# Top-k attention and a squared-ReLU FFN on one core: V laid out by head, a shorter way to the first scores, earlier evacuations in the last steps, and a reordered end

## The chip, the cores and the metric

The kernel runs on one core of one Trainium2 chip. The metric is device time in microseconds (us) of one launch. Of the kernel before there are three timed runs, and one more execution under the hardware profiler. The engines are TensorE (PE, matmuls and, as PEld, weight loads), VectorE (DVE), ScalarE (ACT), GpSimd (POOL) and SyncE (SP, which here issues DMAs).

## The reference

Eight batches of eight heads, 576 positions, 64 numbers per head. For each row of scores only the 32 largest count (and ties with the 32nd); the softmax over them weighs V. The result, 4608 tokens by 512, goes through an FFN with squared ReLU.

```python
scores = scale * np.matmul(q, k.transpose(0, 1, 3, 2))
kth = np.partition(scores, -top_k, axis=-1)[..., -top_k:-top_k + 1]
scores = np.where(scores >= kth, scores, -1000000000.0)
attn = np.exp(scores - np.max(scores, axis=-1, keepdims=True))
attn = attn / (np.sum(attn, axis=-1, keepdims=True) + 1e-09)
x = np.matmul(attn, v)            # then (B*S, H*D)
h = np.maximum(x @ w_in, 0.0)     # w_in 512 x 2048
out = h * h @ w_out               # w_out 2048 x 512
```

## The kernel before

**Units of work.** Heads are taken in 32 pairs, and a pair's 576 query rows in chunks of 128, 128, 128, 128 and 64. A *step* `u` treats one chunk of both heads of a pair, that is two tiles of 128 rows by 576 scores; the chunks of 64 rows of two pairs share a step. There are `U` = 144 steps. In the last batch the four pairs are taken chunk by chunk, so that its tokens come complete one chunk after the other.

**What a step does.** PE multiplies Q by K into the two PSUM tiles `sc_a` and `sc_b` (288 columns each; line 202), ACT copies them to `s` in SBUF (line 207). DVE takes the larger of each pair of columns (`split`, lines 238 to 243), PE brings a part of that back into `sc_b` through an identity matmul (`bring`, line 223), and DVE compares once more (`join`, line 250), so that later rounds look at short windows only. POOL makes the smaller ones by integer sums and differences (lines 257, 265, 269). DVE then finds the 32 largest in four rounds of eight: MAX8 (line 288) over 100, 120, 256 and 576 columns, and MATCH_REPLACE8 (line 292) after each of the first three. In the next step ACT makes `marks` (line 334: what lies below the 32nd) and, earlier, the exponentials `w_two` (`expo`, line 343, one instruction for each of the two tiles); POOL adds the marks to the exponentials as integers (`mask`, line 339); SP turns the result by a transposing DMA into `wT` (line 382); PE multiplies it by V with a column of ones (`weigh`, line 410); DVE inverts the sum (lines 415, 421), and ACT places the result in `x_tok` (line 438).

**Loads.** `load_pair` reads Q, K and V of a pair on SP's queue, one pair ahead of its use. Partition p holds rows 4p to 4p+3 of a head. The SBUF tiles are laid out `[128, chunk 5, head 2, 64]`: the four chunks of a row lie beside each other in DRAM (1 KB), but in SBUF the two heads alternate, so each piece written is 64 float32, 256 B. V's two tiles `v_raw_a` and `v_raw_b` are fixed; POOL casts them (line 154) to `vau`, where a column of ones stands behind each 64 numbers. `prep_units` makes a pair's Q and K ready in units: `main` (line 134) transposes four chunks of Q or K on PE and copies them scaled to `qkT` by ACT (line 138; the very first K by DVE, line 136), `rest` (line 146) does the 64 rows that remain, `values` the cast.

**FFN.** It is woven into the steps as pieces. An `up` (line 512) is a matmul group into one of two PSUM buffers `gen`; its `bend` evacuates by ACT's ReLU into `rl` (line 518) and squares it on POOL (line 526) or, through the list `later`, on ACT (line 523). A `down` (line 540) adds 16 products into `dn_ps`, which `leave` copies to `wide` (line 547) and stores. These evacuations wait in the list `late`; `flush()` issues whatever stands there, and `piece()` flushes before it takes a new piece. `idle_piece` (line 559) is a matmul group without a use, there to keep PE busy. From step `Z` = `U` - 19 on a step ends so:

```python
expo(u, 0)
if u == U - 4:
    piece()
    flush()
expo(u, 1)
flush()
```

**Order.** `pin` keeps each engine's instructions in the order of the program text; the times that `owe` books decide only whether POOL or ACT, DVE or POOL gets certain work.

**The end.** The last step has no later step behind which to hide. Its exponentials (`expo_last`, line 372) come before the 32nd value is known, DVE multiplies them by the comparison (`mask_last`, line 377), PE instead of a DMA transposes them (`turn_last`, lines 392, 395, 397), DVE places the result (`place_last`, line 904). The last 128 tokens get their FFN in quarters of the inner dimension (`x_last(kh)`, lines 884 and 886, and `ups_last(bank, kh)`, line 891, 8 matmuls for each half), collected in `sc_a` and `sc_b`, which are called `one` and `two` there; quarter kh is pair kh of the batch. The last quarter in the order is followed by ReLU (line 896), square (line 898), the `down` matmuls (line 966) and the store. `verify` and `note` (lines 304, 313 to 315) check that the rounds of eight found what they should; lines 947 to 950 sum that up in a flag for a general path, which is not taken here.

Of the kernel before, what the change touches and what calls it, by code (L numbers as in the profile page):

```python
# [22 lines left out]
def kernel(  # L23
# [83 lines left out]
    def load_pair(i):  # L107
        b, pr = pairs[i]
        got = []
        for name, src in (("q_raw", q), ("k_raw", k), ("v_raw", v)):  # L110
            t = ld.tile([128, 5, 2, 64], f32, name=name) if name != "v_raw" else v_raws[i % 2]
            queue = nc.scalar if i == 0 and name == "k_raw" else nc.sync
            two = src[b, 2 * pr:2 * pr + 2]
            if i < 2:
                for a in range(2):
                    pin(queue.dma_start(out=t[:, 0:4, a, :], in_=two[a, 0:512].rearrange("(p c) d -> p c d", c=4)))
            else:
                pin(queue.dma_start(out=t[:, 0:4], in_=two[:, 0:512].rearrange("a (p c) d -> p c a d", c=4)))
            pin(queue.dma_start(out=t[0:64, 4], in_=two[:, 512:576].rearrange("h p d -> p h d")))
            got.append(t)  # L120
        raw[i] = got

    def prep_units(i):
# [5 lines left out]
        def main(which, src):  # L129
            def go():  # L130
                very_first = i == 0 and which == 1
                tp = ps_one.tile([128, 512], f32, name="gen", bufs=2)
                for c in range(4):
                    pin(nc.tensor.transpose(tp[:, c * 128:(c + 1) * 128], src[:, c], id_f[:, :]))
                if very_first:
                    pin(nc.vector.tensor_scalar(qkT[:, which, 0:512], tp[:, :], scalar1=EACH, scalar2=None, op0=ALU.mult))
                else:
                    pin(nc.scalar.activation(qkT[:, which, 0:512], tp[:, :], AF.Copy, scale=EACH))
                    owe(A=0.5)
            return go  # L140
# [10 lines left out]
        def values():  # L151
            owe(G=0.76)
            assert i < 6 or av_left[i - 6] == 0
            pin(nc.gpsimd.tensor_copy(va[:, :, :, 0:64], v_raw[:, :]))
# [494 lines left out]
    scores(0)  # L649
    split(0)  # L650
# [26 lines left out]
    for u in range(Z):  # L677
# [94 lines left out]
    for u in range(Z, U - 2):  # L772
# [40 lines left out]
        if u == U - 4:  # L813
            piece()
            flush()
# [58 lines left out]
    bend()  # L874
    square()
# [12 lines left out]
    def up_last(hp, f0, khs):  # L888
        for kh in khs:
            for n in range(4):  # L890
                pin(nc.tensor.matmul(out=hp[:, n * 128:(n + 1) * 128], lhsT=w_in[:, kh, (f0 + n) * 128:(f0 + n + 1) * 128],
                                     rhs=xl[:, kh, :], start=False, stop=(kh == 2 and n == 3)))
# [26 lines left out]
    bend()  # L919
    square()  # L920
# [179 lines left out]
```

## Time and profile before

| | us |
|---|---|
| Median of three runs | 868.44 |
| Lowest and highest run | 867.41, 871.32 |
| The profiled execution, its own time | 870.59 |
| Its span, first to last instruction | 868.8 |
| First of the 19 last steps (its first exponential) | 735.7 |
| Last MAX8 of DVE ends | 848.2 |
| Last store issued (SP) | 862.75 |

The profile covers one execution. A page of it gives busy time by engine, the chain of work that ended last and the costliest groups of instructions; views of the trace give single instructions in order of time, groups by line, waits, and busy time in chosen stretches. A group's row names line, engine, operation, output and inputs (partitions x elements, type), then count, busy us, mean ns of one, and idle time before it with the instruction that ended it. L288 is line 288 of the kernel.

### The profile page before, as it was taken

How to read it: one execution, taken by the hardware profiler on the slowest of the kernel's cores; microseconds unless marked ns; L12 is line 12 of the kernel's file. 1: busy time of each engine (PE TensorE's matmuls, PEld its weight loads, DVE VectorE, ACT ScalarE, POOL GpSimd, SP SyncE). 2: the span in 40 equal slices, each digit the busy share in tenths (PEclk: the TensorE clock that was granted, in tenths of full speed). 3: DMA queues.
4: the chain of work that ended last, by engine and by line, in shares of the span. 5: the costliest groups of instructions: out<-in, count | busy, mean ns of one | idle time of the engine just before them, and what ended most of it. 6: DMA issues, size and time to landing. Idle time of an engine off the chain costs nothing.

```text
span 868.8 us, 20017 instructions
## 1 busy us (share of the span) xinstructions
PE 761.5 (88%) x6038; PEld 484.6 (56%) x6038; DVE 837.7 (96%) x3427; ACT 810.6 (93%) x1635; POOL 797.5 (92%) x748
## 2 busy tenths in 40 slices
PE   6998997888888988889889888889898998999986
PEld 3554555555555545556555555556555654666654
DVE  5999999999999999999999999999999999999994
ACT  2887999999999999999999999999999999999982
POOL 3788999999999999999999999999999998999761
PEclk8999999999999999999999999999999999999998
DMA  5597776546556666356554565654565545423341
GB/s 122 125 228 156 185 172 109 121 101 114 95 106 114 120 120 121 67 112 121 109 120 96 113 115 98 124 116 105 114 128 109 117 100 107 87 58 86 73 84 44
DMA packets 325444, 98.06 MB, mean 113 GB/s; under 512 B 317520, under 2 KB 317776, under 8 KB 325328
## 3 DMA queue, kind: packets, MB, share of 16 engines
q1 hardware_dynamic: 323984, 96.28, 54.5%
q8 instruction: 49, 0.80, 0.4%
q14 instruction: 67, 0.55, 0.2%
q10 hardware_dynamic: 1344, 0.43, 0.2%
HBM read 36.70 MB, written 9.44 MB: 53 GB/s over the span
## 4 chain that ended last, share of the span: by engine, by line
DVE 56%; issue 12%; POOL 12%; PE 12%; ACT 7%; DMA 1%; SPq 0%; DVEq 0%; ACTq 0%; POOLq 0%
DVE m L288 25%; DVE cat L292 15%; DVE tops L238 7%; DVE cat L250 6%; POOL cat L257 5%; POOL cat L265 3%; ACT s L207 2%; PE sc_b L223 2%; PE sc_b L202 2%; PE gen L512 1%; POOL cat L269 1%; PE av_ps L410 1%; PE dn_ps L559 1%; ACT h L523 1%; PE dn_ps L540 1%
## 5 line engine op out<-in xcount | busy, mean ns | idle before, releaser
L288 DVE MAX8 m<-cat 128x8 f32<-128x100 f32 (+3 forms) x1152 | 435.1, 419 | 0.1
L292 DVE MATCH_REPLACE8 cat<-m,cat 128x100 f32<-128x100 f32 (+2 forms) x864 | 259.3, 308 | 0.3 <-issue 0.3
L265 POOL TENSOR_TENSOR cat<-s 128x576 int32<-128x576 int32 (+1 forms) x144 | 196.1, 1362 | 7.4 <-ACT s L207 7.1
L257 POOL TENSOR_TENSOR cat<-cat,tops 128x576 int32<-128x576 int32 (+1 forms) x144 | 196.0, 1361 | 1.9 <-DVE tops L238 0.8
L202 PE MATMUL sc_b<-qkT 64*128 64x288 f32 (+1 forms) x640 | 119.0, 449 | 33.7 <-DVE cat L250 24.3
L540 PE MATMUL dn_ps<-w_out,h 128*128 128x512 bf16 x560 | 143.3, 381 | 1.9 <-ACT wide L547 1.9
L223 PE MATMUL sc_b<-tops,id_f 128*128 128x144 f32 x528 | 96.6, 306 | 50.5 <-ACT s L207 50.2
L512 PE MATMUL gen<-xT,w_in 128*128 128x256 bf16 (+1 forms) x1088 | 128.5, 264 | 1.9 <-ACT rl L518 1.2
L512 PEld LDWEIGHTS <-w_in 128*128 128x128 bf16 x1344 | 109.9, 98 | 32.8 <-issue 19.9
L223 PEld LDWEIGHTS sc_b<-tops,id_f 128*128 128x128 f32 x528 | 73.4, 189 | 93.8 <-ACT s L207 90.3
L410 PEld LDWEIGHTS <-wT 128*128 128x128 bf16 (+3 forms) x1600 | 98.1, 99 | 47.0 <-issue 8.5
L334 ACT ACTIVATE marks_a<-s,m 128x576 bf16<-128x576 f32 x144 | 115.8, 812 | 0.0
L334 ACT ACTIVATE marks_b<-s,m 128x576 bf16<-128x576 f32 x142 | 110.4, 783 | 0.0
L202 PE MATMUL sc_a<-qkT 64*128 64x288 f32 (+1 forms) x640 | 109.1, 420 | 0.9 <-DVE tops L238 0.9
L207 ACT ACTIVATE s<-sc_b 128x576 f32<-128x576 f32 x144 | 94.8, 659 | 14.0 <-PE sc_b L202 8.6
L207 ACT ACTIVATE s<-sc_a 128x576 f32<-128x576 f32 x144 | 95.9, 666 | 6.6 <-PE sc_a L202 3.8
L238 DVE TENSOR_TENSOR tops<-sc_a,s 128x576 f32<-128x576 f32 x132 | 98.5, 746 | 0.0
L540 PEld LDWEIGHTS <-h 128*128 128x128 bf16 x560 | 47.7, 98 | 68.6 <-issue 31.3
L250 DVE TENSOR_TENSOR cat<-sc_b,tops 128x288 f32<-128x288 f32 x191 | 80.8, 443 | 5.2 <-PE sc_b L223 4.7
L518 ACT ACTIVATE rl<-gen 128x512 f32<-128x512 f32 x140 | 83.9, 599 | 1.0 <-PE gen L512 0.9
L202 PEld LDWEIGHTS sc_b<-qkT 64*128 64x128 f32 (+1 forms) x640 | 48.3, 176 | 61.6 <-DVE cat L250 33.2
L269 POOL TENSOR_TENSOR cat<-tops 128x288 int32<-128x288 int32 x97 | 77.8, 802 | 0.0
(133 smaller groups left out, 1358.4 us busy)
## 6 DMA issues: line engine op xcount, KB each, us to landing
out_dram<-wide SPq DMA_DIRECT2D x31, 256.0 KB, 2.7
q_raw<-in_q_dram SPq DMA_DIRECT2D x30, 256.0 KB, 3.7
k_raw<-in_k_dram SPq DMA_DIRECT2D x30, 256.0 KB, 3.7
h<-in_moe_w_in_dram SPq DMA_DIRECT2D x8, 512.0 KB, 5.3
h<-in_moe_w_out_dram SPq DMA_DIRECT2D x8, 512.0 KB, 4.2
v_raw_a<-in_v_dram SPq DMA_DIRECT2D x15, 256.0 KB, 4.1
v_raw_b<-in_v_dram SPq DMA_DIRECT2D x15, 256.0 KB, 4.0
out_dram<-wide SPq DMA_DIRECT2D x9, 128.0 KB, 2.5
```

The costliest lines, as they stand in the source:

```text
L202: pin(nc.tensor.matmul(out=sc[j][r if rest else slice(0, 128), x, 0:HALF], lhsT=qkT[r, 0, c * 128:min(S, (c + 1) * 128)], rhs=qkT[r, 1, j ...
L207: pin(nc.scalar.activation(s[:, :, j * HALF:(j + 1) * HALF], sc[j][:, :, 0:HALF], AF.Copy))
L223: pin(nc.tensor.matmul(out=far[:, x, :], lhsT=id_f[:, :], rhs=st[w]["tops"][:, x, QUAR:HALF], start=True, stop=True))
L238: pin(tt(tops[:, :, :], one, two, op=ALU.max))
L250: pin(nc.vector.tensor_tensor(d["cat"][:, :, lo:lo + QUAR], far, d["tops"][:, :, 0:QUAR], op=op))
L257: pin(nc.gpsimd.tensor_tensor(at, at, top, op=ALU.subtract))
L265: pin(nc.gpsimd.tensor_tensor(at, s[:, :, 0:n], s[:, :, HALF:HALF + n], op=ALU.add))
L288: pin(nc.vector.max(out=m[r][:, x, :], in_=cat[:, x, at]))
L292: pin(nc.vector.match_replace(out=cat[:, x, at], in_to_replace=m[r][:, x, :], in_values=cat[:, x, at], imm_value=NEG))
L334: pin(nc.scalar.activation(marks[u % 2][:, x, :], d["s"][:, x, :], AF.Relu, bias=d["m"][3][:, x, 7:8], scale=-1.0))
L512: pin(nc.tensor.matmul(out=hp[:, n * n_rows:(n + 1) * n_rows], lhsT=w_in[:, kh, (f0 + n) * 128:(f0 + n + 1) * 128], rhs=xt(kh), start=(kh ...
L540: pin(nc.tensor.matmul(out=op[:, :], lhsT=held["h2"][:, f, c * 128:(c + 1) * 128], rhs=w_out[:, f, :], start=(f == 0), stop=(f == NF - 1)))
```

## The change

It has four parts.

1. V's two tiles become `[128, head 2, chunk 5, 64]`, and a load writes the four chunks of a head as one piece of 1 KB. `values` reads the tile through a rearranged view in the old order.
2. For the first pair, `main` of Q is split: chunk 0 comes first, then K, `rest` and the cast, and chunks 1 to 3 follow the first scores. An `idle_piece` is added in step 0.
3. In the steps from `Z` on, the `flush` between the two exponentials, which was there in one step only, is in all.
4. At the end, both bends that are still open are issued ahead of the last step; the inverse for pair 1 goes between the last two rounds of the last step; `x_last((1,))` and its matmuls, `verify` and `note` go forward; pair 2 comes before pair 3; and quarter 3 instead of quarter 2 is the last.

```diff
-    v_raws = [const.tile([128, 5, 2, 64], f32, name=f"v_raw_{i}") for i in "ab"]
+    v_raws = [const.tile([128, 2, 5, 64], f32, name=f"v_raw_{i}") for i in "ab"]
     for t in v_raws:
-        nc.gpsimd.memset(t[64:128, 4], 0.0)
+        nc.gpsimd.memset(t[64:128, :, 4, :], 0.0)
...
-            t = ld.tile([128, 5, 2, 64], f32, name=name) if name != "v_raw" else v_raws[i % 2]
+            t = ld.tile([128, 5, 2, 64], f32, name=name) if name != "v_raw" else v_raws[i % 2][:, :, :, :].rearrange("p a c d -> p c a d")
...
+                if name == "v_raw":
+                    pin(queue.dma_start(out=v_raws[i % 2][:, :, 0:4, :], in_=two[:, 0:512].rearrange("a (p c) d -> p a c d", c=4)))
+                else:
+                    pin(queue.dma_start(out=t[:, 0:4], in_=two[:, 0:512].rearrange("a (p c) d -> p c a d", c=4)))
...
-        def main(which, src):
+        def main(which, src, c0=0, c1=4):
...
-                for c in range(4):
+                at = slice(c0 * 128, c1 * 128)
+                for c in range(c0, c1):
...
-            return [main(0, q_raw), main(1, k_raw), lambda: rest((1,), sc[0][:, 0, :]), values, lambda: rest((0,))]
+            return [main(0, q_raw, 0, 1), main(1, k_raw), lambda: rest((1,), sc[0][:, 0, :]), values, main(0, q_raw, 1, 4), lambda: rest((0,))]
...
     scores(0)
+    soon.pop(0)()
     split(0)
...
+        if u == 0:
+            idle_piece()
...
         expo(u, 0)
         if u == U - 4:
             piece()
-            flush()
+        flush()
         expo(u, 1)
...
-    bend()
-    square()
+    for _ in range(2):
+        bend()
+        square()
     empty(two)
...
     expo_last(0)
     expo_last(1)
-    bend()
-    square()
     ups_last(one, 0)
     ups_last(two, 0)
     downs.pop(0)()
-    topk(u, (2, 3))
-    invert(u - 2)
+    topk(u, (2,), lambda: invert(u - 2))
+    topk(u, (3,))
     place(u - 2)
+    x_last((1,))
     mask_last(0)
     mask_last(1)
+    verify(u)
+    note()
     turn_last(0)
+    ups_last(one, 1)
     turn_last(1)
-    x_last((1,))
+    products(u - 1)
     st[u]["o"] = ps_one.tile([128, 512], f32, name="gen", bufs=2)[:, 0:130].rearrange("p (x d) -> p x d", x=2)
     products(u)
-    products(u - 1)
+    invert(u - 1)
+    place_last(u - 1)
     invert(u)
     place_last(u)
-    invert(u - 1)
-    place_last(u - 1)
-    x_last((3,))
-    ups_last(one, 1)
     x_last((2,))
     ups_last(two, 1)
-    ups_last(one, 3)
-    ups_last(two, 3)
-    verify(u)
-    note()
+    x_last((3,))
+    ups_last(one, 2)
+    ups_last(two, 2)
...
-        ups_last(bank, 2)
+        ups_last(bank, 3)
```

More of the change, by code (lines that the diff above doesn't have):

```diff
@@ L132, in go @@
                 tp = ps_one.tile([128, 512], f32, name="gen", bufs=2)
[L133 removed]
+                at = slice(c0 * 128, c1 * 128)
+                for c in range(c0, c1):
                     pin(nc.tensor.transpose(tp[:, c * 128:(c + 1) * 128], src[:, c], id_f[:, :]))
                 if very_first:
[L136 removed]
+                    pin(nc.vector.tensor_scalar(qkT[:, which, at], tp[:, at], scalar1=EACH, scalar2=None, op0=ALU.mult))
                 else:
[L138 removed]
+                    pin(nc.scalar.activation(qkT[:, which, at], tp[:, at], AF.Copy, scale=EACH))
                     owe(A=0.5)
@@ L891, in up_last @@
                 pin(nc.tensor.matmul(out=hp[:, n * 128:(n + 1) * 128], lhsT=w_in[:, kh, (f0 + n) * 128:(f0 + n + 1) * 128],
-                                     rhs=xl[:, kh, :], start=False, stop=(kh == 2 and n == 3)))
+                                     rhs=xl[:, kh, :], start=False, stop=(kh == KH - 1 and n == 3)))
     def square_last(z, bank):
```

3 lines of the change are left out of this document (1 added, 2 removed).

## The prediction

> **What bounds the kernel now.** I read the page first: which engine is busy, and how evenly. VectorE (DVE) leads, with ScalarE (ACT) and GpSimd (POOL) close behind.
>
> ```profile
> span 868.8 us, 20017 instructions
> ...
> PE 761.5 (88%) x6038; PEld 484.6 (56%) x6038; DVE 837.7 (96%) x3427; ACT 810.6 (93%) x1635; POOL 797.5 (92%) x748
> ```
>
> A busy share is a mean over stages, so the second view is busy time by stretch. Behind the length of a stretch each row gives busy us and instructions of PE, PEld, DVE, ACT and POOL, then the granted TensorE clock, the DMA share and GB/s.
>
> ```profile
> 0.00:10.00 10.00, 7.35 (x27) 3.51 (x27) 0.84 (x2) 2.75 (x4) 3.85 (x23) 1.00 0.67 144
> ...
> 100.00:600.00 500.00, 435.80 (x3447) 277.76 (x3448) 498.80 (x2054) 492.61 (x993) 495.04 (x455) 1.00 0.57 113
> 735.00:806.00 71.00, 67.54 (x574) 45.65 (x574) 66.07 (x274) 68.07 (x144) 69.57 (x64) 0.98 0.35 72
> 806.00:848.20 42.20, 38.78 (x380) 25.09 (x380) 41.98 (x182) 37.08 (x78) 29.48 (x30) 1.00 0.39 84
> 848.20:868.80 20.60, 12.09 (x121) 9.46 (x119) 8.40 (x19) 5.19 (x14) 2.09 (x4) 0.87 0.14 40
> ```
>
> From 100 to 600 us DVE is idle for 500 - 498.80 = 1.2 us: nothing is to be won there without taking DVE work away, and the change takes none. DVE's idle time lies in three places: the first 10 us (9.2 us), 735 to 806 us (71 - 66.07 = 4.9 us) and behind 848.2 us (20.6 - 8.4 = 12.2 us). Set beside the old one, engine by engine, the new order of instructions differs in just these places, and in the shape of V's loads. So there are four parts.
>
> **V in pieces of 1 KB: nothing.** Instruction groups (count | busy us, mean ns | idle before), then DMA issues (count, KB, median us to landing):
>
> ```profile
> L607 POOL CAST w_in<-h 128x1024 bf16<-128x1024 f32 x5 | 5.2, 1039 | 0.0
> ...
> L154 POOL CAST vau_a<-v_raw_a 128x640 bf16<-128x640 f32 x6 | 4.4, 727 | 3.5 <-DMA v_raw_a<-in_v_dram 3.5
> ```
> ```profile
> out_dram<-wide SPq DMA_DIRECT2D x31, 256.0 KB, 2.7
> ...
> v_raw_b<-in_v_dram SPq DMA_DIRECT2D x15, 256.0 KB, 4.0
> ```
>
> A store of 256 KB in rows of 2 KB lands in 2.7 us, a load of V in pieces of 256 B in 4.0 us: at best each load lands 1.3 us sooner. The one wait for V in the profile is POOL's 3.5 us ahead of its first cast, before POOL has other work, and load_pair runs a pair ahead. That lead is the cover; without it each of the 32 pairs could win those 1.3 us, or lose up to a landing. I take 0. The cast (L154) now reads in nested steps (chunk, head, 64 numbers) where it read 640 numbers in a row. From the two casts above, 384 more numbers cost 312 ns, 0.8 ns each, so 640 come to 0.52 us and 0.2 us is fixed; the output of L154 is in runs of 64 already and shows no price for them. I take the new cast at 0.73 us too; the bounds are that and double (a rival, below).
>
> **The start: -0.55 us.** Timeline rows: start us, length us, engine, line, and in brackets the idle time before and what ended it.
>
> ```profile
> 6.04 1.02 PE L134 MATMUL gen<-id_f,q_raw 128*128 128x128 f32 x4 [0.28 <-DMA q_raw<-in_q_dram]
> ...
> 6.90 0.60 PE L134 MATMUL gen<-id_f,k_raw 128*128 128x128 f32 x4
> ...
> 7.54 0.69 DVE L136 TENSOR_SCALAR qkT<-gen 128x512 f32<-128x512 f32 x1 [7.54 <-PE gen L134]
> ...
> 9.85 0.47 DVE L240 TENSOR_TENSOR sc_b<-sc_a,s 128x288 f32<-128x288 f32 x1 [1.62 <-ACT s L207]
> ...
> 11.13 0.65 ACT L207 ACTIVATE s<-sc_a 128x576 f32<-128x576 f32 x1 [1.32 <-DVE cat L243]
> ...
> 15.45 1.33 PE L202 MATMUL sc_b<-qkT 64*128 64x288 f32 x4 [2.28 <-ACT qkT L149]
> ...
> 18.46 0.47 DVE L240 TENSOR_TENSOR sc_b<-sc_a,s 128x288 f32<-128x288 f32 x1 [0.39 <-ACT s L207]
> ```
> ```profile
> L134 PE MATMUL gen<-id_f,k_raw 128*128 128x128 f32 x128 | 20.7, 284 | 0.6 <-ACT rl L518 0.6
> ```
> ```profile
> 14.00:21.00 7.00, 5.50 (x17) 2.49 (x18) 6.61 (x26) 2.06 (x4) 3.17 (x4) 0.53 0.56 126
> ```
>
> K's four transposes now stand behind one of Q's instead of four. Q's four took (6.90 - 6.04) / 4 = 0.215 us apiece; K's four took 0.60 with one of them lasting 0.28, so a step of (0.60 - 0.28) / 3 = 0.11: the clock rose in between. Three fewer are 0.645 us if K's keep their pace, but they would now run before the rise: four steps of 0.215 and 0.28 for the fifth end at 7.18 instead of 7.50, 0.32 sooner. I take 0.35, since the rise seems to go by time; the bounds are 0.32 and 0.645. All behind it (L136, the scores, L207, DVE's first L240) moves along. The other three transposes and their copy by ACT (384 columns, under the 0.60 us of 512) go behind the first scores, into the 1.32 us for which ACT waits ahead of its copy at 11.13: free; without that gap up to 0.6.
>
> The added idle_piece (four matmuls of 512) lands in the 2.28 us for which PE waits before 15.45: free up to that. It may keep the clock up through 14 to 21 us, where the mean was 0.53 and the scores took 1.33 us. Then DVE's 0.39 us at 18.46 goes. I take 0.2, bounds 0 and 0.39.
>
> **The last 19 steps: -1.2 us.** A flush now comes between the two exponentials in every step, so the waiting evacuation (L518 or L547) precedes the second one.
>
> ```profile
> 735.73 1.44 ACT L343 ACTIVATE w_two_c<-s,low 128x576 bf16<-128x576 f32 x2
> ...
> 737.08 0.57 ACT L547 ACTIVATE wide<-dn_ps 128x512 f32<-128x512 f32 x1
> ...
> 737.71 1.86 PE L559 MATMUL dn_ps<-fill,id_h 128*128 128x512 bf16 x4 [0.58 <-ACT wide L547]
> ...
> 742.91 0.46 DVE L250 TENSOR_TENSOR cat<-sc_b,tops 128x288 f32<-128x288 f32 x1 [0.47 <-PE sc_b L223]
> ...
> 751.02 1.03 PE L512 MATMUL gen<-xT,w_in 128*128 128x256 bf16 x8 [0.59 <-ACT rl L518]
> 751.05 1.04 POOL L526 TENSOR_TENSOR h<-rl 128x512 bf16<-128x512 f32 x1 [0.44 <-ACT rl L518]
> ...
> 755.73 0.82 DVE L250 TENSOR_TENSOR cat<-sc_b,tops 128x288 f32<-128x288 f32 x2 [0.69 <-PE sc_b L223]
> ```
> ```profile
> 800.96 1.02 PE L540 MATMUL dn_ps<-w_out,h 128*128 128x512 bf16 x4 [0.64 <-ACT wide L547]
> ...
> 805.61 0.82 DVE L250 TENSOR_TENSOR cat<-sc_b,tops 128x288 f32<-128x288 f32 x2 [0.93 <-PE sc_b L223]
> ```
>
> Three times PE waits for an evacuation behind the second exponential (0.58, 0.59, 0.64 us), then scores late, and DVE waits at its next L250 (0.47, 0.69, 0.93). The evacuation comes one exponential, 0.72 us, sooner; each stall shrinks by the smaller number, together 0.47 + 0.59 + 0.64 = 1.7 us. The second exponential is 0.6 us later. Behind it on ACT are the placing and the marks; POOL's addition to the weights waits for the marks, which end when they did, since the order only rotates ACT's work. That is the cover; without it the turn, and PE's products, would be 0.6 us late. But POOL is idle for only 71 - 69.57 = 1.4 us of this stretch and ACT for 2.9: they can take the bound over. I take 1.2, bounds 0 and 1.7.
>
> **The tail: -2.0 us.** The first row has the shortest, median and longest of two instructions, in ns.
>
> ```profile
> L377 DVE SCALAR_TENSOR_TENSOR w_two_c<-s,m,marks_b x2: 797/1196/1594, 848.2 to 848.9; 128x576 bf16<-128x576 f32 x2
> ```
> ```profile
> 846.26 1.04 POOL L526 TENSOR_TENSOR h<-rl 128x512 bf16<-128x512 f32 x1
> ...
> 848.59 1.31 POOL L526 TENSOR_TENSOR h<-rl 128x512 bf16<-128x512 f32 x1 [1.29 <-ACT rl L518]
> ...
> 850.57 0.45 PE L392 MATMUL gen<-id_h,w_two_c 128*128 128x128 bf16 x5 [1.06 <-DVE w_two_c L377]
> ...
> 853.60 0.29 PE L884 MATMUL gen<-id_h,x_tok 128*128 128x128 bf16 x1
> 853.68 1.06 PE L891 MATMUL sc_b<-xT,w_in 128*128 128x128 bf16 x8
> 854.53 1.06 PE L891 MATMUL sc_a<-xT,w_in 128*128 128x128 bf16 x8
> ...
> 857.21 1.08 ACT L896 ACTIVATE rl<-sc_a 128x512 f32<-128x512 f32 x2 [3.01 <-PE sc_a L891]
> ```
> ```profile
> 847.09 0.61 PE L891 MATMUL sc_b<-xT,w_in 128*128 128x128 bf16 x8
> ```
> ```profile
> 850.00:853.40 3.40, 2.47 (x35) 1.95 (x35) 1.79 (x6) 0.79 (x3) 0.00 (x0) 1.00 0.00 0
> 853.40:856.80 3.40, 3.40 (x34) 3.21 (x32) 1.89 (x6) 0.29 (x2) 0.78 (x3) 0.50 0.00 0
> ```
>
> mask_last(1) took 1.594 us beside POOL's square of 848.59, mask_last(0) 0.797. With both bends ahead of the last step that square follows the one of 846.26 and ends at 846.26 + 2 x 1.04 = 848.3, so the second mask should take 0.80 too: 0.8 us, and the transposes of 850.57 wait that much less. The new order then lets pair 2's product run while DVE copies the last transposed weights, and puts one group of eight L891 into PE's 1.06 us wait and a second between the two x_tok transposes: three groups, not four, stand between the last L884 and the first ReLU (L896). A group takes 854.53 - 853.68 = 0.85 us at half clock. Of that and the reordering I count 0.65 (the second group may hold up the last L884 by 0.3), so 0.8 + 0.65 = 1.45 us at half clock. At full clock eight take 0.61 in place of 1.06 (row of 847.09), so three groups win 3 x 0.45 = 1.35 more: 2.8. Between 1.45 and 2.8 no row decides: PE is busier than before, yet the clock fell after 3.4 us in which PE was busy for 2.47. I take 2.0. The flag checks move forward; DVE does them while PE runs L891, as before.
>
> The Trainium skill, page "TensorE: Matmul & The Clock Gate", section "Part 1: The HAM clock gate (the "warmup" mystery)", says that the clock is halved after an idle window of some 3.4 us, whose phase varies from run to run. The row of 850 to 853.4 us speaks against a wholly idle window as the condition; by the page the tail would keep its clock, as in the second rival.
>
> **Sum.** 0.55 + 1.2 + 2.0 = 3.75 us off the profiled execution's own 870.59 us (span 868.8 and 1.8 around it) are 866.84. That execution is 2.15 us above the median of the three runs, 868.44; against the median the forecast is 864.7 us.
>
> **Rivals.** First, the engines behind take over: POOL and ACT are the bound in the last 19 steps (for it, 69.57 of 71 us; against it, two of POOL's waits there are for the same L518) and the clock falls as before. 0.35 + 0 + 1.45 = 1.8 us: 866.6. Second, the clock stays full in both places: 0.35 + 0.39 + 1.2 + 2.8 = 4.7 us: 863.7. Third, slower: the nested read makes POOL's cast cost double. From 100 to 600 us POOL is idle for 500 - 495.04 = 5 us, over some 20 casts 0.25 us each; past that POOL becomes the bound, and 0.73 - 0.25 = 0.48 us on some 25 casts of the filled stage cost 12 us: 868.44 - 3.75 + 12 = 876.7. Against it is the price of runs of 64 above. That the 1 KB pieces do nothing for the time is no rival but part of all four.
>
> **How the numbers follow.** Forecast 0.45, first rival 0.22, second 0.20, third (with any other loss) 0.13. Lowest sum of all bounds: 1.03 + 1.7 + 2.8 = 5.5 us; three runs spread by some 2 us to each side. Range 861 to 869.5: from below the second rival to no gain at all with that spread; the third is left out. Half a per cent (4.3 us, about what a measurement of this kernel can tell from no change) lies at 864.1, just past the forecast. Faster by more: 0.65 of the second rival and half of the forecast's cases, 0.35; slower 0.12; the rest, 0.53, within.
>
> **What would show it.** K's transposes end near 7.2 us and DVE's first L240 starts near 9.5. The three L250 waits are below 0.4 us together with their PE waits gone; if POOL's idle time there falls to nothing while DVE's stays at 4.9, the first rival holds. Both L377 take 0.8 us; L896 starts 1.4 to 2.8 us sooner against the end of the last maximum. L154 stays at 0.73 us: above 1 us the third rival holds. A DVE idle time above 1.2 us between 100 and 600 us would prove the forecast wrong.

## The result, and the profile after

| | before | after |
|---|---|---|
| median of five runs each, side by side | 869.83 us (867.41 to 871.32) | 865.07 us (864.59 to 865.77) |
| ratio, 95% interval | | 0.9946 (0.9924 to 0.9968) |
| later, on one chip: 18 and 7 runs | 870.13 us (866.79 to 873.70) | 864.81 us (863.57 to 865.31) |
| ratio, 95% interval | | 0.9931 (0.9908 to 0.9955) |
| span of the profiled execution | 868.8 us | 863.3 us |

The change makes the kernel faster by 4.8 to 5.3 us. The forecast was 864.7 us. Lines behind the change have moved: old L134, L136, L154, L202, L207, L223, L240, L250, L377, L410, L518 and L896 are L138, L140, L158, L206, L211, L227, L244, L254, L381, L414, L522 and L904 in the changed kernel.

The page of the changed kernel, its head and the busy times, and then the same stretches as before, cut at the new end of the last maximum:

```profile
span 863.3 us, 19942 instructions
...
PE 754.1 (87%) x5960; PEld 483.8 (56%) x6042; DVE 836.9 (97%) x3427; ACT 810.0 (94%) x1636; POOL 797.2 (92%) x748
```
```profile
0.00:10.00 10.00, 7.19 (x26) 3.46 (x27) 0.86 (x2) 2.43 (x4) 3.85 (x23) 0.89 0.66 146
100.00:600.00 500.00, 431.71 (x3401) 277.93 (x3445) 498.64 (x2052) 492.09 (x992) 494.76 (x455) 1.00 0.55 113
735.00:806.00 71.00, 67.08 (x585) 46.32 (x594) 67.78 (x279) 69.51 (x148) 70.67 (x65) 1.00 0.38 74
806.00:846.80 40.80, 37.33 (x356) 23.82 (x359) 40.62 (x178) 35.87 (x76) 29.60 (x30) 1.00 0.44 88
846.80:863.30 16.50, 10.32 (x119) 7.97 (x119) 7.41 (x17) 4.61 (x12) 0.78 (x3) 0.94 0.26 46
```

Between 100 and 600 us nothing moved (DVE busy for 498.64 us, 498.80 before). From 735 to 806 us DVE, ACT and POOL are all busier, so the same work takes less time. The last stretch is 16.5 us long where it was 20.6. In the first 10 us the mean clock is given as 0.89, where it was 1.00, but these two cannot be compared: the time ahead of the clock's first rise counts as full in them. The rise came at 6.86 us before and at 4.45 us after, and the ten matmuls of the warm-up show it, first in the kernel before and then in the changed one (0.43 us from one to the next ahead of the rise, 0.21 behind it):

```profile
1.31 4.45 PE L620 MATMUL dn_ps<-fill 128*128 128x512 bf16 x10 [1.31 <-POOL fill L73]
```
```profile
1.31 3.86 PE L624 MATMUL dn_ps<-fill 128*128 128x512 bf16 x10 [1.31 <-POOL fill L73]
```

The timeline of DVE at the start of the changed kernel (only instructions behind a wait), and the clock by windows of 3.41 us, show what comes behind the rise:

```profile
6.78 0.69 DVE L140 TENSOR_SCALAR qkT<-gen 128x512 f32<-128x512 f32 x1 [6.78 <-PE gen L138]
9.84 0.47 DVE L244 TENSOR_TENSOR sc_b<-sc_a,s 128x288 f32<-128x288 f32 x1 [2.36 <-PE sc_a L206]
14.30 0.47 DVE L244 TENSOR_TENSOR sc_b<-sc_a,s 128x288 f32<-128x288 f32 x1 [0.89 <-PE sc_a L206]
19.16 0.47 DVE L244 TENSOR_TENSOR sc_b<-sc_a,s 128x288 f32<-128x288 f32 x1 [0.18 <-ACT s L211]
```
```profile
4.45:7.86 3.41, 1.91 (x12) 1.03 (x11) 0.69 (x1) 0.50 (x2) 0.59 (x1) 1.00 0.84 186
7.86:11.27 3.41, 2.69 (x11) 1.39 (x9) 1.43 (x4) 1.33 (x3) 0.17 (x2) 0.50 0.68 174
11.27:14.69 3.42, 2.79 (x10) 1.56 (x11) 2.54 (x16) 1.09 (x2) 1.58 (x2) 0.50 0.05 11
14.69:18.10 3.41, 3.36 (x13) 1.61 (x10) 3.41 (x12) 1.25 (x3) 1.59 (x2) 0.50 0.07 16
```

DVE's copy of K (L140) starts at 6.78 us, 0.76 sooner than the 7.54 of before. But the clock falls to half at 7.9 us and stays there for three windows, and DVE's first L244 is where it was (9.84 against 9.85); the third is 0.7 us later (19.16 against 18.46). From step 3 on, the two executions are level (0.02 us apart). The gain of the start is gone.

At the other end, rows of the last 19 steps and of the tail of the changed kernel, from the timelines of DVE, PE, ACT and SP's DMA queue:

```profile
804.05 0.82 DVE L254 TENSOR_TENSOR cat<-sc_b,tops 128x288 f32<-128x288 f32 x2 [0.27 <-PE sc_b L227]
...
846.68 1.53 DVE L381 SCALAR_TENSOR_TENSOR w_two_c<-s,m,marks_b 128x576 bf16<-128x576 f32 x2
...
849.37 0.79 PE L414 MATMUL av_ps<-vau_a,wT 128*128 128x65 bf16 x10 [0.65 <-DMA wT<-w_two_b]
...
853.14 1.08 ACT L904 ACTIVATE rl<-sc_a 128x512 f32<-128x512 f32 x2 [1.12 <-PE sc_a L899]
...
858.68 0.34 SPq L979 DMA_DIRECT2D out_dram<-wide  x1
```
The masks and the last store's issue of the kernel before, from the same timelines:

```profile
848.20 2.31 DVE L377 SCALAR_TENSOR_TENSOR w_two_c<-s,m,marks_b 128x576 bf16<-128x576 f32 x2
...
862.75 0.33 SPq L973 DMA_DIRECT2D out_dram<-wide  x1
```

From the first mask to the last store's issue it took 862.75 - 848.20 = 14.55 us and now takes 858.68 - 846.68 = 12.00 us; the two masks together take 1.53 us in place of 2.31. The ReLU at 853.14 (L904) was at 857.21 (L896). By stages, with the start of the first maximum of a step as the mark, the two profiled spans (868.81 and 863.30) part like this:

| stretch | before | after | difference |
|---|---|---|---|
| to the last 19 steps (step 125) | 731.38 | 731.67 | +0.29 |
| steps 125 to 142 | 107.69 | 105.84 | -1.85 |
| step 142 to the first mask | 9.13 | 9.17 | +0.04 |
| first mask to the last store's issue | 14.55 | 12.00 | -2.55 |
| last store's issue to the end | 6.06 | 4.62 | -1.44 |

The first row is not the start. The two executions stay level up to step 23; the difference comes at step 24, during a window of half clock from 151.2 to 154.6 us that only the changed kernel's execution has. (Steps 20 to 29 take 57.60 or 57.61 us in the six profiles here without a fall near 150 us, and 57.82 to 57.93 us in the eight with one.) The last row is no part of the change: in other profiles of the kernels here it lies between 4.6 and 5.8 us, with no pattern. V's casts and landings, a group and a DMA row of the changed kernel:

```profile
L158 POOL CAST vau_a<-v_raw_a 128x640 bf16<-128x640 f32 x6 | 4.3, 724 | 3.5 <-DMA v_raw_a<-in_v_dram 3.5
```
```profile
v_raw_b<-in_v_dram SPq DMA_DIRECT2D x15, 256.0 KB, 3.8
```

The nested read costs the cast nothing (724 ns against 727), and pieces of 1 KB land 0.2 us sooner (3.8 against 4.0), which nothing waits for.

So the time agrees with the forecast while its terms do not: the start gained nothing where 0.55 us were forecast, and the rest gained more. What the order did and what the clock did is the question for the runs.

### The profile page after: what moved, and what is told of

Its sections match the earlier page's. It is cut to its first block, busy times and chain, and to the rows that moved or that the text cites. A ratio compares the mean times of both kernels' runs of the same rounds, so it can differ in the third digit from the quotient of the medians.

```text
span 863.3 us, 19942 instructions
## 1 busy us (share of the span) xinstructions
PE 754.1 (87%) x5960; PEld 483.8 (56%) x6042; DVE 836.9 (97%) x3427; ACT 810.0 (94%) x1636; POOL 797.2 (92%) x748
## 4 chain that ended last, share of the span: by engine, by line
DVE 53%; PE 17%; issue 11%; POOL 11%; ACT 6%; DMA 1%; SPq 0%; DVEq 0%; ACTq 0%; POOLq 0%
DVE m L292 23%; DVE cat L296 14%; DVE tops L242 7%; DVE cat L254 6%; POOL cat L261 4%; POOL cat L269 3%; PE sc_b L227 3%; PE sc_b L206 2%; PE gen L516 2%; PE av_ps L414 2%; PE dn_ps L544 2%; ACT s L211 2%; PE sc_a L206 2%; PE dn_ps L563 2%; POOL cat L273 1%
## 5 line engine op out<-in xcount | busy, mean ns | idle before, releaser
L206 PE MATMUL sc_b<-qkT 64*128 64x288 f32 (+1 forms) x640 | 119.7, 452 | 31.8 <-DVE cat L254 25.5
L227 PE MATMUL sc_b<-tops,id_f 128*128 128x144 f32 x528 | 96.5, 305 | 50.0 <-ACT s L211 49.4
L544 PE MATMUL dn_ps<-w_out,h 128*128 128x512 bf16 x492 | 131.7, 380 | 7.2 <-issue 3.5
L227 PEld LDWEIGHTS sc_b<-tops,id_f 128*128 128x128 f32 x528 | 73.5, 189 | 92.6 <-ACT s L211 89.0
L414 PEld LDWEIGHTS <-wT 128*128 128x128 bf16 (+3 forms) x1600 | 97.9, 99 | 48.9 <-issue 8.0
L206 PE MATMUL sc_a<-qkT 64*128 64x288 f32 (+1 forms) x640 | 110.9, 426 | 0.9 <-DVE tops L242 0.9
L211 ACT ACTIVATE s<-sc_b 128x576 f32<-128x576 f32 x144 | 94.9, 659 | 13.4 <-PE sc_b L206 6.8
L211 ACT ACTIVATE s<-sc_a 128x576 f32<-128x576 f32 x144 | 96.0, 667 | 6.4 <-PE sc_a L206 4.5
L522 ACT ACTIVATE rl<-gen 128x512 f32<-128x512 f32 x140 | 84.1, 601 | 0.9 <-PE gen L516 0.9
L254 DVE TENSOR_TENSOR cat<-sc_b,tops 128x288 f32<-128x288 f32 x191 | 80.8, 444 | 2.9 <-PE sc_b L227 2.3
L206 PEld LDWEIGHTS sc_b<-qkT 64*128 64x128 f32 (+1 forms) x640 | 48.3, 176 | 58.4 <-DVE cat L254 32.8
```

What stands on the lines that cost most here:

```text
L206: pin(nc.tensor.matmul(out=sc[j][r if rest else slice(0, 128), x, 0:HALF], lhsT=qkT[r, 0, c * 128:min(S, (c + 1) * 128)], rhs=qkT[r, 1, j ...
L211: pin(nc.scalar.activation(s[:, :, j * HALF:(j + 1) * HALF], sc[j][:, :, 0:HALF], AF.Copy))
L227: pin(nc.tensor.matmul(out=far[:, x, :], lhsT=id_f[:, :], rhs=st[w]["tops"][:, x, QUAR:HALF], start=True, stop=True))
L254: pin(nc.vector.tensor_tensor(d["cat"][:, :, lo:lo + QUAR], far, d["tops"][:, :, 0:QUAR], op=op))
L544: pin(nc.tensor.matmul(out=op[:, :], lhsT=held["h2"][:, f, c * 128:(c + 1) * 128], rhs=w_out[:, f, :], start=(f == 0), stop=(f == NF - 1)))
```

## The experiments

My theory at this point: the reordering is worth some 3 us, and the remainder is clock. Between executions the kernel before spends very different times at half clock; worked out as (1 - mean granted clock) x 2 x span it is 20.6 us as a mean of its 18 runs beside the changed kernel's second measurement, and 12.6 us in the changed kernel. (This counts the time ahead of the first rise as full, and it includes the last few us, where the clock falls once more behind the last store's issue.) The rival: the order of the work is the whole gain, and the clock a bystander.

### The four parts, each alone on the kernel before

V's layout and loads alone, then the start alone:

```
-    v_raws = [const.tile([128, 5, 2, 64], ...)]
+    v_raws = [const.tile([128, 2, 5, 64], ...)]
...
+    pin(queue.dma_start(out=v_raws[i % 2][:, :, 0:4, :], in_=two[:, 0:512].rearrange("a (p c) d -> p a c d", c=4)))
```

> The kernel before with V's layout alone. My theory (the landing is hidden, the cast costs the same): within 0.5 us of the kernel before, casts at 0.72 us, landings of V about 0.4 us sooner. The rival of the costlier cast: casts near 1.4 us and some 12 us slower. A rival by relieved DMA queues: 1 us or more faster.

```
-    return [main(0, q_raw), main(1, k_raw), ...]
+    return [main(0, q_raw, 0, 1), main(1, k_raw), ..., main(0, q_raw, 1, 4), ...]
...
     scores(0)
+    soon.pop(0)()
...
+        if u == 0:
+            idle_piece()
```

> The kernel before with the split first transposes and the added idle matmuls alone. My theory as forecast: 0.55 us faster (0.3 to 1.0). The rival drawn from the changed kernel's profile: the TensorE clock falls somewhere in the first 20 us whatever stands there, at a phase that differs from run to run, so the median moves by less than 0.5 us to either side and DVE's third L240 (step 2) starts between 18.0 and 19.5 us.

The flush between the two exponentials alone, then the tail alone (both bends ahead of the last step, and the new order):

```
             piece()
-            flush()
+        flush()
         expo(u, 1)
```

> The kernel before with the flush between the exponentials in all of the last 19 steps, alone. My theory: 1.2 to 1.9 us faster; DVE's waits ahead of its joins (0.47, 0.69, 0.93 us) shrink to 0.3 or less, its two waits for the products of the 64-row steps (0.94 and 1.02 us) stay. The rival that POOL and ACT take over as the bound: under 0.5 us.

```
-    bend()
-    square()
+    for _ in range(2):
+        bend()
+        square()
...
     turn_last(0)
+    ups_last(one, 1)
     turn_last(1)
-    x_last((1,))
+    products(u - 1)
...
```

> The kernel before with the reordered end alone. My theory: 2.0 to 2.8 us faster; both mask instructions at 0.80 us; the first ReLU of the last tokens 2.5 us sooner after DVE's last maximum than before. The rival that the gain of the changed kernel's profile was the phase of the clock: at half clock 1.45 us, so 1.2 to 1.6 us faster, and the eight matmuls of a group at 1.06 us.

Twelve runs of each, beside 35 of the kernel before (median 870.02 us):

| part alone | median | ratio, 95% interval |
|---|---|---|
| V's layout | 870.53 us | 1.0012 (0.9993 to 1.0032) |
| start | 868.41 us | 0.9976 (0.9956 to 0.9996) |
| flush | 869.86 us | 0.9998 (0.9980 to 1.0017) |
| tail | 868.77 us | 0.9982 (0.9962 to 1.0003) |

V is worth nothing. The others cannot be told apart: a part of 1 us is no larger than its interval, for the runs of the kernel before alone spread over 7 us. By their medians they add up to 2.5 us (+0.5, -1.6, -0.2, -1.2), half of what the whole change gains; the start gave more than expected, the flush and the tail less. The profiles say more than the times. With one window of 3.4 us at half clock in each, steps 125 to 142 took 107.69 us in the kernel before and 106.06 us with the flush alone.

### The changed kernel without its start; the tail in halves

The changed kernel with the start put back:

> The changed kernel with the start put back as it was (all of Q's transposes ahead of K's, no added idle_piece): V's layout, the flush and the tail stay. Theory 'the parts add up': alone, V's layout, the flush and the tail were worth +0.3, -0.8 and -1.5 us as means, so about -2 us against the kernel before, ratio 0.997 to 0.998. Rival 'the start is worth nothing in the whole', as the profiled pair has it, whose first step came out 0.29 us later after the change: this kernel keeps all that the changed kernel gained, -4.8 us, ratio 0.9945.

866.11 us, ratio 0.9961 (0.9942 to 0.9981): between the two expectations, and the interval holds both. (The 0.29 us that the expectation puts on the start are those of step 24.) Only a run that takes the clock out can decide this one (below).

The kernel before with both bends early and nothing else, and with the new order of the tail but the last bend where it was:

```
     turn(u)
-    bend()
-    square()
+    for _ in range(2):
+        bend()
+        square()
...
     expo_last(1)
-    bend()
-    square()
```

> The kernel before with nothing but both last evacuations and squares moved ahead of the last step. Theory 'the second mask was slow because it ran beside POOL's square': both masks take 0.80 us, and the ReLU behind them comes 0.8 us sooner at the same clock; time -0.8 us and what the clock of the run adds, ratio 0.998 to 1.000. Rival 'the second mask is slow by itself (its operands)': 0.8 and 1.6 us as before, ratio 1.000.

```
     expo_last(1)
     bend()
     square()
...
     turn_last(0)
+    ups_last(one, 1)
     turn_last(1)
-    x_last((1,))
+    products(u - 1)
...
```

> The kernel before with the tail's new order of PE work and checks, but the last evacuation and square left where they were. Theory: the masks stay at 0.8 and 1.6 us; from the end of the last maximum to the last store's issue it takes 0.65 to 1.2 us less than the 13.08 us at full clock of the old order, 11.9 to 12.4 at full clock; ratio 0.998 to 0.9995. Rival 'the order is worth nothing without the sooner mask': 13.1 us at full clock, ratio 1.000.

They took 867.88 us (0.9976, 0.9952 to 1.0000) and 867.88 us (0.9973, 0.9952 to 0.9994). The second did what was expected: the masks stay at 0.8 and 1.6 us, and from the first mask to the last store's issue it takes 13.91 us in place of the 14.55 of the kernel before, with one window of half clock in each: 0.64 us for the order, although PE waited 0.40 us for a transposing DMA in it and not at all in the kernel before. The first did not: moving the square did not make both masks fast, it made the other one slow. The group of masks and the timeline of DVE and POOL with the bends alone early, and behind them the same rows with V's layout alone, where nothing was moved:

```profile
L377 DVE SCALAR_TENSOR_TENSOR w_two_c<-s,m,marks_b x2: 805/1087/1369, 846.5 to 847.8; 128x576 bf16<-128x576 f32 x2
```
```profile
845.22 2.03 POOL L526 TENSOR_TENSOR h<-rl 128x512 bf16<-128x512 f32 x2
846.50 2.10 DVE L377 SCALAR_TENSOR_TENSOR w_two_c<-s,m,marks_b 128x576 bf16<-128x576 f32 x2
```
```profile
847.60 1.55 DVE L380 SCALAR_TENSOR_TENSOR w_two_c<-s,m,marks_b 128x576 bf16<-128x576 f32 x2
...
848.79 1.26 POOL L529 TENSOR_TENSOR h<-rl 128x512 bf16<-128x512 f32 x1 [1.51 <-ACT rl L521]
```

With the bends early the squares end at 847.25, and the first mask, begun at 846.50 under the second square, ends at 847.87, 0.62 us behind it. In the kernel before, the second mask ends at 850.51, 0.61 us behind the square's end at 849.90. In four more profiles it is 0.61 to 0.62. In the other direction, with V alone, the second mask was already running when the square came: the masks took 0.82 and 0.81 us, and the square 1.26 in place of 1.04. Whichever starts first keeps its pace and the other waits. The Trainium skill, page "SBUF — State Buffer", section "SBUF: two separate sides", says that VectorE and GpSimd hold a port pair in common as an exclusive lock that goes to the one that starts first, among others between a VectorE instruction with two inputs in SBUF and a GpSimd instruction that reads SBUF. Who waits for whom agrees; a mask that waited in full would end 0.80 us behind the square, and the six ends lie 0.61 to 0.62 us behind it.

In the changed kernel the squares end at 846.72, 0.04 us into the first mask, and the masks take 0.80 and 0.81 us; so it is in all six profiles that have the flush and the new tail. With the bends alone the same edit only moves the collision, and from the first mask to the last store's issue it takes 13.05 us at full clock, against 13.06 for the old order at full clock (below): nothing won. The flush is not what decides, though. The tail alone has no flush, and there too the squares end 0.04 us into the first mask:

```profile
848.64 2.04 POOL L526 TENSOR_TENSOR h<-rl 128x512 bf16<-128x512 f32 x2
850.64 1.53 DVE L377 SCALAR_TENSOR_TENSOR w_two_c<-s,m,marks_b 128x576 bf16<-128x576 f32 x2
```

In that execution DVE had waited 2.04 us ahead of its L250 at 745.29, at the end of a stretch of half clock, and in the last step POOL's work stands 0.93 us further ahead of DVE's last maximum than with the bends alone. Whether the flush or such a wait sets this was not separated.

And a quick mask is worth little in the old order. With V's layout alone both masks were quick, and the last store was issued here:

```profile
860.55 0.34 SPq L976 DMA_DIRECT2D out_dram<-wide  x1
```

From the first mask to this row it took 860.55 - 847.60 = 12.95 us at full clock, 0.11 us less than the 13.06 with a slow second mask. The last transposed weights were ready 0.77 us sooner, but PE's products with them came only 0.42 us sooner, and the next ones waited 0.25 us for a transposing DMA that landed 5.09 us behind its issue; without that wait it would have been 0.36 us, an estimate.

### Taking the clock out

When does the clock fall? It changes only on a grid of 3.413 us: in the kernel before at 6.862, 13.689 and 20.515 us, then at 737.314 us, whole numbers of such windows apart. Thirteen profiles of these kernels and a fourteenth of the last run below, cut on that grid from 3 to 855 us, give:

```
PE busy in a window at full clock, us   windows   half clock in the next
below 1.6                                 19        18
1.6 to 1.8                                 5         3
1.8 to 2.1                               101        12
2.1 to 2.4                               196         0
2.4 to 2.7                               478         2
above 2.7                               2645         0

PE busy in a window at half clock, us   windows   full clock in the next
below 2.9                                 13         0
2.9 to 3.2                                11         9
above 3.2                                 27        25
```

(PE's busy time can be a little short here: the page of the changed kernel has 5960 matmuls and 6042 weight loads.) The clock does not wait for an idle window: in 33 of 35 cases it fell after windows in which PE was busy for a third to three fifths of the time. The kernel before has a fall in three places: behind windows at 10 us, at 734 us and at 850 us. The second of them and the one behind it, in its windows:

```profile
733.90:737.30 3.40, 2.03 (x18) 1.30 (x17) 3.19 (x12) 3.37 (x10) 3.40 (x4) 1.00 0.71 101
737.30:740.70 3.40, 2.99 (x10) 1.32 (x11) 3.40 (x19) 2.66 (x8) 3.31 (x7) 0.50 0.58 125
```

Whether a fall comes there depends on where the grid lies, which differs from run to run. The test is to fill these windows with idle matmuls. First in the start of the changed kernel:

```
-    for n in range(10):
+    for n in range(13):
...
+    idle_piece(3)
     scores(0)
     soon.pop(0)()
+    idle_piece(5)
...
         if u == 0:
-            idle_piece()
+            idle_piece(7)
```

> The changed kernel with more idle matmuls on TensorE in the first 16 us (3 more in the warm-up, 3 ahead of the first scores, 5 behind them, 7 in place of 4 in the first step), each where TensorE waits. Theory 'time at half clock costs time': the half clock of the first 20 us (10.2 us long in the changed kernel's profile) goes or shortens to 3.4 us, the maxima of the third step start at 18.0 to 18.3 us in place of 19.2, and the time falls by 1 to 2.8 us below the changed kernel: ratio to the kernel before 0.991 to 0.9935. Rival 'the order sets the time and the clock is a bystander': the clock stays up and the time stays at the changed kernel's 0.9945, or is 0.5 to 1 us longer because the added matmuls stand ahead of needed ones.

DVE in the start of this kernel:

```profile
9.52 0.47 DVE L244 TENSOR_TENSOR sc_b<-sc_a,s 128x288 f32<-128x288 f32 x1 [1.65 <-ACT s L211]
13.06 0.47 DVE L244 TENSOR_TENSOR sc_b<-sc_a,s 128x288 f32<-128x288 f32 x1
17.66 0.45 DVE L244 TENSOR_TENSOR sc_b<-sc_a,s 128x288 f32<-128x288 f32 x1
```

The half clock of the start is gone, and the third L244 comes at 17.66, 1.5 us sooner than the 19.16 of the changed kernel, more than expected. The time, 865.39 us and ratio 0.9950 (0.9930 to 0.9970), does not show it; its runs spread from 862.78 to 868.21 us, and the profiled one fell to half clock at 736.5 us. So the next three ran side by side. The changed kernel as it is:

> The changed kernel as it is, beside the next two on one chip. Theory: 865 to 866 us, ratio 0.994 to 0.996, as in its first runs; half clock, where it falls, in the first 20 us and at 737 us in some executions and not in others. If the ratio is above 0.998, the first measurement of the change was chance.

The changed kernel, filled in the start as above and also at 734 us:

```
         if not piece():
             idle_piece()
+        if u == Z:
+            idle_piece(4, "gen", 2)
         bring(u + 2)
```

> The changed kernel with the added idle matmuls of the first 16 us, and four more in the first of the last 19 steps, where TensorE waits 1.1 us for ScalarE's copies. Theory 'time at half clock costs time': no half clock in the first 20 us nor at 737 us; 1 to 2 us less than the changed kernel beside it, ratio to the kernel before 0.992 to 0.9935. Rival 'only the order counts': the same time as the changed kernel beside it, or up to 0.5 us more for the added matmuls.

The kernel before, its order untouched, filled in all three places (with the longer warm-up and the edit at `u == Z` of the last two, not shown again):

```
...
+    idle_piece(3)
     scores(0)
+    idle_piece(8)
...
+        if u == 0:
+            idle_piece(8)
...
     turn_last(0)
+    for n in range(4):
+        pin(nc.tensor.matmul(out=one[:, n % 2, :], lhsT=zero[:, :], rhs=fill[:, :], start=False, stop=False))
     turn_last(1)
```

> The kernel before, its order of work untouched, with idle matmuls where TensorE waits: in the first 16 us, in the first of the last 19 steps, and four products with zero weights (added to a bank that collects the tail's sums, which they leave as they are) ahead of the last transposed weights. Theory 'half of the gain is clock': the half clock goes in all three places, from the end of the last maximum to the last store's issue it takes 13.1 us (as with a full clock in another run of the old tail) in place of 14.5 to 15.6, and the kernel takes 867 to 868 us, ratio 0.996 to 0.998, with a narrower spread than the kernel before. Rival 'the order is the gain': the time stays at the kernel before's, ratio 1.000, or rises by the added matmuls.

| | median | ratio, 95% interval | mean half clock |
|---|---|---|---|
| kernel before | 870.13 us (866.79 to 873.70) | | 20.6 us |
| before, filled | 866.41 us (865.28 to 867.62) | 0.9957 (0.9940 to 0.9973) | 7.8 us |
| changed kernel | 864.81 us (863.57 to 865.31) | 0.9931 (0.9908 to 0.9955) | 12.6 us |
| changed, filled | 863.23 us (862.91 to 865.05) | 0.9922 (0.9896 to 0.9948) | 7.2 us |

The old order with nothing but idle matmuls is 3.7 us faster, and its spread shrinks from 7 to 2.3 us: the clock is no bystander. What half clock is left lies elsewhere, most often behind a window at 146 to 148 us, in eight of the fourteen profiles. Between the two filled kernels lie 866.41 - 863.23 = 3.2 us, the worth of the new order with the clock up; the changed kernel still has 864.81 - 863.23 = 1.6 us to win from the clock. So its gain of 5.3 us is 3.2 us of order and 3.7 - 1.6 = 2.1 us of clock. These are differences of medians, and they take the added matmuls to cost the same in both orders. The runs of the two filled kernels do not overlap (865.28 us and up, 865.05 us and down), so the order has a part for certain; those of the changed kernel with and without filling do, so the 1.6 us, and with it the split, is less certain. A second way agrees: among the 18 runs of the kernel before, a straight line gives 0.31 us for each us at half clock, and the 8.0 us less in the changed kernel would be 2.5 us.

The two filled kernels, old order first, from the first mask to the last store's issue, and steps 125 to 142 by their stretch and the old order's stalls there:

```profile
742.28 0.79 PE L410 MATMUL av_ps<-vau_c,wT 128*128 128x65 bf16 x10 [1.44 <-DMA wT<-w_two_b]
...
750.68 1.03 PE L512 MATMUL gen<-xT,w_in 128*128 128x256 bf16 x8 [0.59 <-ACT rl L518]
...
755.38 0.82 DVE L250 TENSOR_TENSOR cat<-sc_b,tops 128x288 f32<-128x288 f32 x2 [0.69 <-PE sc_b L223]
...
847.85 2.32 DVE L377 SCALAR_TENSOR_TENSOR w_two_c<-s,m,marks_b 128x576 bf16<-128x576 f32 x2
...
860.91 0.33 SPq L981 DMA_DIRECT2D out_dram<-wide  x1
```
```profile
735.00:806.00 71.00, 66.22 (x579) 44.92 (x578) 65.75 (x273) 67.95 (x143) 69.36 (x63) 1.00 0.35 71
```
```profile
845.38 1.53 DVE L381 SCALAR_TENSOR_TENSOR w_two_c<-s,m,marks_b 128x576 bf16<-128x576 f32 x2
...
847.25 0.78 PE L414 MATMUL av_ps<-vau_a,wT 128*128 128x65 bf16 x10
...
856.54 0.34 SPq L983 DMA_DIRECT2D out_dram<-wide  x1
```
```profile
735.00:806.00 71.00, 68.47 (x608) 46.72 (x608) 67.70 (x286) 69.54 (x147) 70.68 (x65) 1.00 0.38 75
```

The tail takes 860.91 - 847.85 = 13.06 us in the old order and 856.54 - 845.38 = 11.16 in the new one, both at full clock: the new end as a whole, order and early squares together, is worth 1.9 us. In the changed kernel's own profile 0.65 us of that are given back to a new wait (the row of 849.37 above): the transposing DMA of the step before the last landed 4.6 us behind its issue, here 3.5 us, and the filled kernel's row of 847.25 has no wait. Five profiles of the new tail take 11.35, 11.34, 11.35, 11.35 and 11.17 us when that wait (0.65, 0.72, 0.68, 1.16 and none) is taken off; the last run below takes 11.25 us without one.

Steps 125 to 142 take 107.93 us in the old order and 105.83 in the new one. In the old order a late transposing DMA (1.44 us at 742.28) turned into the stalls of 750.68 and 755.38, which the half clock had caused in the kernel before. In two profiles of the old order in which neither came (V's layout alone and the bends alone), it took 106.66 us and 106.59 us; PE's wait of 0.59 us is gone there without the flush, and DVE's of 0.69 us is 0.22 and 0.23, while the one of 0.93 us at the end of the stretch stays. The flush is therefore worth 0.8 us when nothing is late, and up to 2.1 us when something is.

The last run has the old order in the start, and all else of the filled changed kernel:

> The changed kernel with the start put back as it was (all of Q ahead of K) and the idle matmuls of the first 16 us and of the first of the last 19 steps added: the kernel of the run before last in all but the start's order. Theory 'the start's order is worth what three transposes take, and the rest of its effect is clock': with the clock up, the ten first steps take the same 35.0 us behind K's copy, and the time is that of its counterpart with the new start, ratio 0.992, or 0.3 us more. Rival 'the new order of the start is worth 1.5 us', as the runs without it had it: ratio 0.994.

```profile
7.30 0.69 DVE L139 TENSOR_SCALAR qkT<-gen 128x512 f32<-128x512 f32 x1 [7.30 <-PE gen L137]
```

863.69 us, ratio 0.9915 (0.9892 to 0.9938), from five runs. (A sixth execution took 3754.3 us; whether it went through the general path, and why, is open, so this version is not put forward.) The first maximum of step 5, the sixth step (the ten steps of the expectation are a miscount), starts at 42.27 us here, at 42.38 with the new start filled, and at 42.14 in the filled old kernel; behind DVE's copy of K (7.30, 7.40 and 7.16 us) that is 34.97, 34.98 and 34.98 us. With the clock up the two starts are alike: what the new one can win is the time of three transposes, 0.33 us at full pace, and in the filled kernel with the new start the warm-up held Q back by a little more (its first transpose at 6.65 us, here at 6.23). In the changed kernel the same stretch takes 43.68 - 6.78 = 36.90 us, with 10.2 us at half clock in it.

## Why the prediction came out, step by step

The range held and the forecast was close, but that is in part luck: of its four steps V's was right, the start's failed, and the other two gained somewhat more than their terms, in part for other reasons.

- V: right. Neither the landings nor the nested cast are seen in the time, alone or with the rest.
- The start, -0.55 us: the step that failed. The copy of K came 0.76 us sooner, past the bound of 0.645, since the clock of that execution had risen at 4.5 us already and the four Q transposes of before (1.02 us) had met it low. That the added idle_piece "may keep the clock up" failed: it stands at 14 us, and the clock had fallen at 7.9 us, after a window in which PE was busy for 1.91 us. In the profiled pair the start is worth nothing (0.02 us from step 3 on); alone it was worth 1.6 us by its median, with the clock at half for less long (14.9 us as a mean against 22.1). With the clock taken out it is worth nothing that can be measured.
- The last 19 steps, -1.2 us: right in kind, too small. The three L250 stalls shrank as described (0.47, 0.69 and 0.93 us became none, 0.12 and 0.27), and POOL's two waits went with them; the stretch gained 1.85 us, just over the bound of 1.7. But the first two of these stalls were not a lasting part of the old order, as the prediction took them to be: they came behind half clock at 737 us or a late DMA, and without either only the third is the flush's own, 0.8 us for the stretch. The 1.2 us lie between that and the 2.1 us. The first rival was wrong in part: POOL now has 0.33 us of idle time in the 71 us, yet the stretch did get shorter.
- The tail, -2.0 us: right in sum, not in its terms. At full clock the new end is worth 1.9 us, where 0.8 for the mask and 0.65 for the order, 1.45 us, were taken at half clock. The order alone gave the 0.64 us above. The 0.8 us of the mask exist as a collision, but they did not reach the end of the old order: with both masks quick it was 0.11 us shorter. How the 1.9 us part between the order and the early squares beside it was not separated. A fresh wait for a DMA took up to 1.2 us of it away, which no step had named. And the clock, which the sum had halfway, stayed full: one window of half clock in the old tail is 14.55 - 13.06 = 1.5 us.
- The second rival (the clock full in both places) was half true: full at the end, half at the start.
- The sum: 3.75 us were forecast from the profiled execution. The pair gave 5.5 us, of which 1.44 lie behind the last store's issue and are not of the change. Against the three runs' median the forecast landed 0.4 us off; with more runs the kernel before has a median near 870 us, and the gain is some 1 to 1.5 us larger than forecast. The base of three runs was 1.4 to 1.7 us too low, the gain about as much too small, and the two cancelled: the closeness is luck.

What stays open: why the clock fell in only 12 of the 101 windows with 1.8 to 2.1 us of PE work; why the same transposing DMA lands anywhere from 3.5 to 5.1 us behind its issue; what sets POOL's place beside DVE at the end, and with it which of mask and square starts first; and what made two runs of the kernel before take 874 us with 12 us of half clock, since neither was profiled.

## What to carry to other kernels

A change of half a per cent is no larger than what the clock of TensorE does from run to run: before the parts of a small gain are argued over, look up in which windows the clock fell, and compare stages at the same clock. What half clock costs depends on the stage: one window of it cost 1.5 us in the old tail, 0.3 us at step 24. Where PE has to wait anyway, idle matmuls cost little and can be worth as much as a reordering: here 3.7 us for some 30 of them, and 863.23 us for the changed kernel filled at the start and at 734 us, the lowest median of all. An evacuation placed ahead of the work that does not need it is worth most where something else comes late.

## What the runs showed of the hardware

- The granted clock of TensorE fell to half after windows of 3.413 us in which PE was busy for 1.1 to 2.1 us (two of 35 times for 2.4 to 2.6), and came back after windows with 2.9 us or more, 34 times of 38 (the table above). The Trainium skill, page "TensorE: Matmul & The Clock Gate", section "Part 1: The HAM clock gate (the "warmup" mystery)", puts the fall behind an idle window; the length and the free-running grid agree with the runs, the idle window does not: 35 falls before 855 us came behind windows with PE busy for 1.1 us or more.
- A mask of DVE that starts 0.75 to 0.99 us ahead of the end of a POOL square ends 0.61 to 0.62 us behind it, in six profiles, and takes 1.37 to 1.61 us in place of 0.80; a square that starts under a mask takes 1.26 to 1.36 us in place of 1.04.
